# A planned attention and feed-forward kernel: smaller feed-forward steps, other TensorE prices, and a rearranged start

## The chip, the cores and the metric

One NeuronCore of one Trainium2 chip runs the whole program. The metric is the device time of one execution in microseconds (us); lower is better. Three executions of the kernel before took 1087.53, 1088.04 and 1089.18 us, so its median is 1088.04 us. A further execution was profiled; every row below comes from it.

## The reference, cut to what matters

```
scores = scale * q @ k.T                         # 8 batches x 8 heads, 576 tokens, head size 64
scores = where(block_i >= block_j, scores, -1e9) # blocks of 64 tokens
attn   = exp(scores - max(scores)); attn /= sum(attn) + 1e-9
x      = attn @ v                                # (batch, 576, 512)
u      = x + ((x.T @ U) @ V).T                   # U 576 x 32, V 32 x 576
out    = u + relu(u @ w_ch1) @ w_ch2             # 512 -> 2048 -> 512
```

Inputs of the attention and the results are float32; U, V and the two weight matrices arrive as float64.

## The kernel before, in words

**Two stages.** In the first, the 64 heads go through attention one after the other, and 768 of the 2048 hidden columns of the feed-forward part are computed beside them, in 16 chunks of 288 tokens (`ffn_chunk`). In the second stage (`block_products`) the other 1280 hidden columns follow as block products with seven multiplications in place of eight, 3360 TensorE products at L905.

**A head.** SP fetches q and k transposed (`split_qk`); ACT or DVE rounds them into `qa` and `kk`, POOL or DVE makes the remainders `qb` and the second half of `kk`, and two small DMAs copy the halves to the other partitions. Rows 64 to 100 of `qa` and `kk` hold marks of the blocks, so that the mask is part of the product. `maxima` forms the masked scores on TensorE (L1255, L1257), DVE takes their row maxima into `mx` (L1264), TensorE turns `mx` around (L1271), ACT or DVE copies it into `mr`, and a DMA on SP (L1281) lays it into row 96 of `qa`, which subtracts the maximum inside the next product. `probabilities` makes the scores again in three groups (L1300, L1301) and ACT takes their exponential; `apply_v` multiplies with v (L1350 for the first ten heads in float32, L1354 to L1356 afterwards in three 16-bit products); each second head is followed by `mix`, which applies U and V.

**Weights.** `split64` reads 64-bit words by a DMA into a staging buffer `st`, then one ACT, one POOL and three DVE steps make float32 of them. U and V go through it first, then the first 768 columns' w1 (`first_w1`), w2, and all other weights.

**Who sets the order.** Every step of the first and second stage is given to `Plan.add` with an engine, a price in ns, a priority, a function that emits the instructions, and what it reads and writes. `Plan.issue` plays the program with these prices: whenever an engine falls free, it takes the ready step of smallest priority number that it can start. The order found is emitted as it is, and each engine then works through its own list in order; an instruction whose semaphore is not there yet holds up all behind it. Feed-forward products have priorities from 1e6 on, so TensorE takes them when no attention step is ready, in steps of `GM` products of 288 columns. Until 260 us of planned time, `idle` puts products on a tile of zeros (L1495) where TensorE has nothing at all. `START` says when each engine is free for the first time, `VARIANT` seeds a spread of 4% on all prices, and `INTO` is the time that a result takes to reach another engine.

TensorE's steps are priced by `_pe`, for which each product takes its columns, or 109 ns if that is more, with 40 or 60 ns on top in the caller:

```
m = [*m, *[P] * len(ns)][1 : len(ns)] + [P]
return sum(max(0.85 * w, n * COL) for n, w in zip(ns, m))
```

Of the kernel before, what the change touches and what calls it, by code (L numbers as in the profile page):

```python
# [56 lines left out]
START = {"PE": 5000, "DVE": 5600, "ACT": 2750, "POOL": 5500, "SP": 700}  # L57
COL = 0.4555
LA, VA, MP = 1100,700,500
# [13 lines left out]
LIFT = 8  # L73
FW = 10
# [89 lines left out]
class Plan:  # L164
# [8 lines left out]
    def add(self, engine, ns, prio, fn, reads=(), writes=(), hold=(), after=0, port=False, others=(), lazy=False):  # L173

        n = len(self.tasks)
        k = 1 + 0.04 * ((n * 40503 + 7919 * VARIANT) % 65536 / 65536 - 0.5)
# [10 lines left out]
        slots = {b for b in (*reads, *writes) if b.pool is not None}  # L187
# [3 lines left out]
        self.tasks.append(Task(ways, prio, deps, after, slots))  # L191
        if lazy:
            self.tasks[-1].goal = "lazy"

    def issue(self, tc):
# [10 lines left out]
        port, held, last = False, 0, None  # L206
        taken = [False] * len(tasks)
# [13 lines left out]
        while done < len(tasks):  # L221
            for e, q in ready.items():
# [18 lines left out]
                for x in later:  # L241
                    heapq.heappush(q, x)
                spare = [p[-1] for p in self.banks if p]
# [61 lines left out]
def _pe16(*ns):  # L305
    return sum(2.4 + 0.4167 * n for n in ns)


def _pe(*ns, m=()):

    m = [*m, *[P] * len(ns)][1 : len(ns)] + [P]
    return sum(max(0.85 * w, n * COL) for n, w in zip(ns, m))
# [3 lines left out]
def attention_then_mixer(  # L316
# [58 lines left out]
    st_r = ring(fp, 2, [P, GF, 2], I32, "st")  # L375
    z_r = ring(fp, 2, [P, GF], I32, "z")

    def split64(fetches, shape, hi, lo, dst, prio, gate=(), part=slice(None), whole=None):
# [34 lines left out]
        add("SP", max(630 * len(fetches), 2.85 * n), prio, fetch, gate, [st], after=4500 if whole else DL)  # L413
# [12 lines left out]
        add("ACT", _act(n, True), prio, lambda: nc.scalar.copy(hi(), zf), [zt], [dst])  # L426
        add("POOL", 60 + 2.3 * n, prio, lambda: nc.gpsimd.tensor_sub(lo(), zf[part], f32(hi()[part])), [zt, dst], [dst])
# [18 lines left out]
    def power(mu, n, by, sc, prio, pool):  # L446
# [9 lines left out]
            "PE", 150, prio,  # L456
# [579 lines left out]
    nc.scalar.activation(warm.ap, warm.ap, AF.Exp)  # L1036

    for _ in range(9):
        nc.tensor.matmul(banks_f[0][:, 0:P], zero.ap, zero.ap, start=True, stop=True)
# [26 lines left out]
    marks = buf(ap, [P, 2 * W], F32, "marks")  # L1066
# [6 lines left out]
    nc.vector.memset(marks[low], 0.0)  # L1073
    nc.vector.memset(marks[96:101, W : 2 * W], 1.0)
    for n, fill in enumerate((1.0, NEG)):
        x = marks[64:96, n * W : (n + 1) * W].rearrange("p (i h c) -> p i h c", i=5, h=2)
        for h, base in ((1, 0), (0, -5)):
            nc.gpsimd.affine_select(
                out=x[:, :, h, :], in_=x[:, :, h, :], pattern=[[-1, 5], [0, 64]], compare_op=ALU.not_equal,
                fill=fill, base=base, channel_multiplier=1,  # L1080
            )
    make_identity(nc, ident.ap)
    nc.vector.memset(f32(qa_r[0][0:64, 0:64]), 0.0)
    nc.vector.memset(f32(kk_r[0][0:64, :, S:W]), 0.0)
    nc.vector.memset(f32(kk_r[0][64:P, 1, S:W]), 0.0)
    for n in range(2):
        nc.vector.memset(pl_r[n][:, PW - 64 :], 0.0)
        nc.vector.memset(vw(n)[:, :, D : D + 1], 1.0)
    nc.vector.tensor_copy(qa_r[0][low], marks[low, 0:W])
    nc.vector.tensor_copy(kk_r[0][low, 0, :], marks[low, W : 2 * W])  # L1090

    def masked(n, pr):
# [3 lines left out]
        def pads():  # L1096
            nc.gpsimd.memset(f32(qa[0:64, 0:64]), 0.0)
            nc.gpsimd.memset(f32(kk[0:64, :, S:W]), 0.0)
            return nc.gpsimd.memset(f32(kk[64:P, 1, S:W]), 0.0)

        add("POOL", 500, pr, pads, [], [qa.parts[0], *kk.parts])
        for to, x, b in ((qa[low], 0, qa.parts[0]), (kk[low, 0, :], W, kk.parts[0])):
            add(
                "ACT", _act(W, True), pr, lambda to=to, x=x: nc.scalar.copy(to, marks[low, x : x + W]), [], [b],
                others=[("DVE", 64 + 0.55 * W, lambda to=to, x=x: nc.vector.tensor_copy(to, marks[low, x : x + W]), True, 300)],
            )

    def mixing_weights(prio):


        def fetch_u(t):
# [6 lines left out]
            [fetch_u], [P, 4, R], lambda: ust[:, 0:4, 0:R], lambda: ust[:, 0:4, R : 2 * R], ust.parts[0], prio  # L1118
        )
        split64(  # L1120
            [
                lambda t, j=j: nc.sync.dma_start(
                    out=t[64 * j : 64 * (j + 1)], in_=U[512:576, :].rearrange("p (r t) -> p r t", t=2)
                )
                for j in range(2)
            ],
            [P, R], lambda: ust[:, 4, 0:R], lambda: ust[:, 4, R : 2 * R], ust.parts[1], prio,
        )
        for a in (0, T):
            split64(  # L1130
                [
                    lambda t, j=j, a=a: nc.sync.dma_start(
                        out=t[R * j : R * (j + 1)], in_=V[:, 2 * a : 2 * (a + T)].rearrange("p (s t) -> p s t", t=2)
                    )
                    for j in range(3)
                ],
                [3 * R, T], lambda a=a: v3[:, a : a + T], lambda a=a: v3[2 * R :, a : a + T], v3.parts[a // T], prio,
                part=slice(2 * R, 3 * R),
            )

    def split_qk(h, pr):
# [395 lines left out]
```

## Time and profile before

| | us |
|---|---|
| median of three executions | 1088.04 |
| profiled execution | 1086.81 |
| its span, first to last instruction | 1084.9 |
| TensorE busy | 1059.7 (98%) |
| VectorE busy | 965.4 (89%) |
| ScalarE busy | 691.4 (64%) |
| mean granted TensorE clock | 0.997 |

The profiled execution lies 1.9 us over its span and 1.2 us under the median. Matmuls overlap in the pipeline and their ends are modelled, so a TensorE that reads as busy may still lose time between products; the distance from one start to the next tells more than a duration. PE is TensorE's products, PEld its weight loads, DVE VectorE, ACT ScalarE, POOL GpSimd, SP the engine that issues DMAs.

### The profile page before, as it was taken

What the parts mean: (1) busy time and instruction counts of PE and PEld (TensorE: products, weight loads), DVE (VectorE), ACT (ScalarE), POOL (GpSimd) and SP (SyncE); (2) the same over time, 40 slices, a digit from 0 to 9 for tenths busy, and PEclk for the clock granted to TensorE, in tenths of its full rate; (3) what the DMA queues carried; (4) which work ended last, traced back from release to release, by engine and by line L of the source; (5) the groups of instructions that cost most, each with busy time, mean ns of one, the idle gap of its engine ahead of it and who ended that gap; (6) DMA issues with size and microseconds to landing.
All of it is one profiled execution on the core that took longest, in us unless ns stands there. A gap on an engine that the chain in (4) does not pass through costs nothing.

```text
span 1084.9 us, 27041 instructions
## 1 busy us (share of the span) xinstructions
PE 1059.7 (98%) x10325; PEld 891.8 (82%) x10325; DVE 965.4 (89%) x1999; ACT 691.4 (64%) x1435; POOL 405.1 (37%) x509
## 2 busy tenths in 40 slices
PE   9999999999999999999999999999999999999998
PEld 8888888888888878878878877777777777777776
DVE  8899999999999999989988525899998989898987
ACT  5569786777778877867887423455454545455553
POOL 5446566657358886657688330000000000000000
PEclk9899999999999999999999999999999999999999
DMA  8674646565464675555354377040404040313111
GB/s 197 180 198 120 176 118 182 145 190 160 121 193 145 176 220 170 154 171 170 112 174 147 123 264 244 29 132 2 131 1 132 10 123 22 111 34 99 44 46 44
DMA packets 87041, 141.33 MB, mean 130 GB/s; under 512 B 9664, under 2 KB 60800, under 8 KB 86912
## 3 DMA queue, kind: packets, MB, share of 16 engines
q1 hardware_dynamic: 86912, 139.61, 44.3%
q8 instruction: 81, 1.33, 0.5%
q14 instruction: 48, 0.39, 0.1%
HBM read 83.05 MB, written 37.49 MB: 111 GB/s over the span
## 4 chain that ended last, share of the span: by engine, by line
PE 52%; DVE 26%; ACT 6%; DMA 4%; POOL 3%; issue 3%; SPq 0%; DVEq 0%; POOLq 0%; ACTq 0%
PE bb L905 38%; DVE mx L1264 5%; DVE pp L1330 5%; PE bf L612 4%; PE bf L636 3%; DMA vr<-in_v_dram 2%; DVE z L398 2%; DVE hl L620 1%; PE bg L636 1%; DVE wr L406 1%; POOL wr L734 1%; DVE ot L648 1%; DVE x L1369 1%; POOL sg L730 1%; DVE vm L1193 1%
## 5 line engine op out<-in xcount | busy, mean ns | idle before, releaser
L905 PEld LDWEIGHTS <-wb 128*128 128x128 f16 x3360 | 328.7, 98 | 83.2 <-issue 0.3
L905 PE MATMUL bb<-hh,wb 128*128 128x288 f16 x2240 | 370.8, 286 | 0.0
L905 PE MATMUL bb<-hl,wb 128*128 128x288 f16 x1120 | 238.2, 286 | 0.2 <-DVE hl L843 0.2
L834 ACT CAST hh<-hb 128x576 f16<-128x576 f32 (+1 forms) x96 | 56.7, 591 | 66.8 <-PE bb L905 65.6
L636 PE MATMUL bf<-hh,w2h 128*128 128x288 f16 x336 | 96.9, 288 | 0.2 <-DVE hl L620 0.2
L636 PE MATMUL bf<-hh,w2l 128*128 128x288 f16 x336 | 96.2, 286 | 0.0
L636 PE MATMUL bf<-hl,w2h 128*128 128x288 f16 x336 | 96.2, 286 | 0.0
L860 DVE TENSOR_TENSOR wr<-bb,wr 128x576 f32<-128x576 f32 (+1 forms) x120 | 78.0, 654 | 15.7 <-PE bb L905 15.7
L636 PEld LDWEIGHTS <-w2h 128*128 128x128 f16 x768 | 75.1, 98 | 20.5 <-issue 1.3
L612 PEld LDWEIGHTS <-w1h 128*128 128x128 f16 x768 | 72.0, 98 | 21.9 <-issue 4.1
L1264 DVE TENSOR_REDUCE mx<-ba 128x1 f32<-128x320 f32 (+1 forms) x188 | 85.4, 479 | 1.7 <-PE ba L1257 1.6
L1354 PE MATMUL ba<-vv,pp 128*128 128x65 f16 x810 | 85.2, 193 | 0.5 <-DVE tz L1403 0.5
L1355 PE MATMUL ba<-vv,pp 128*128 128x64 f16 x810 | 84.9, 195 | 0.0
L1356 PE MATMUL ba<-vv,pp 128*128 128x65 f16 x810 | 84.2, 192 | 0.2
L1163 POOL TENSOR_TENSOR qb<-raw,qa 64x576 fp32r<-64x576 f32 x48 | 67.5, 1405 | 42.1 <-ACT qa L1156 16.3
L1355 PEld LDWEIGHTS <-pp 128*128 128x128 f16 x810 | 75.3, 97 | 1.7 <-issue 0.7
L1354 PEld LDWEIGHTS <-pp 128*128 128x128 f16 x810 | 74.7, 96 | 2.2 <-issue 0.2
L1356 PEld LDWEIGHTS <-pp 128*128 128x128 f16 x810 | 75.3, 99 | 0.5 <-DVE pp L1330 0.4
L1330 DVE TENSOR_TENSOR pp<-ba,pp 128x512 f16<-128x512 f32 (+1 forms) x107 | 67.5, 643 | 2.8 <-ACT pp L1325 2.8
L612 PE MATMUL bf<-uh,w1l 128*128 128x288 f16 x368 | 69.4, 287 | 0.0
L834 ACT CAST hh<-wr 128x576 f16<-128x576 f32 (+1 forms) x72 | 42.6, 592 | 39.9 <-PE bb L905 39.9
L838 ACT ACTIVATE hh<-ur,sc 128x576 f16<-128x576 f32 x46 | 35.6, 776 | 50.4 <-PE bb L905 28.7
(221 smaller groups left out, 2869.7 us busy)
## 6 DMA issues: line engine op xcount, KB each, us to landing
raw<-in_qk_dram SPq DMA_DIRECT2D x63, 288.0 KB
vr<-in_v_dram SPq DMA_DIRECT2D x32, 320.0 KB
qb<-qa SPq DMA_DIRECT2D x64, 144.0 KB
kk<-kk SPq DMA_DIRECT2D x64, 144.0 KB
o_d<-ot SPq DMA_DIRECT2D x64, 144.0 KB
wr<-o_d SPq DMA_DIRECT2D x32, 288.0 KB
wb<-w_d SPq DMA_DIRECT2D x14, 640.0 KB
out_dram<-wr SPq DMA_DIRECT2D x31, 288.0 KB
```

What stands on the lines that cost most here:

```text
L612: nc.tensor.matmul(ps[:, :T], w()[wn][:, k, fs], m[k].ap, start=(i == 0), stop=(i == len(ops) - 1))
L636: nc.tensor.matmul(ps[:, :T], w()[wn][:, f, ms], hs[f][x].ap, start=(i == 0), stop=(i == len(ops) - 1))
L834: add("ACT", _act(size(x), True), E, lambda: nc.scalar.copy(h(), x[0]()), [x[1]], [hb])
L838: "ACT", _act(size(x), True) + 105, E, lambda: nc.scalar.activation(h(), x[0](), AF.Copy, scale=sc[:, 0:1]), [x[1], sc],
L860: add("DVE", _dve(size(out)), E, lambda: getattr(nc.vector, op)(out[0](), x[0](), y[0]()), [x[1], y[1]], [out[1]])
L905: nc.tensor.matmul(bank[:, i, :T], w(x, k), p.ap[:, k, :], start=first and n == 0, stop=last and n == len(ops) - 1)
L1163: sub = lambda e, dst=dst, x=x, y=y: lambda: e.tensor_sub(dst, raw[:, x], f32(y))
L1264: lambda i=i, view=view: nc.vector.tensor_reduce(out=mx[:, i : i + 1], in_=view(), op=ALU.max, axis=AX.XY if i == 4 else AX.X, negate=True,),
L1330: lambda at=at, view=view, shaped=shaped: nc.vector.tensor_sub(shaped(pl[:, at]), view(), shaped(ph[:, at])),
L1354: nc.tensor.matmul(bank[:, o : o + D + 1], ph[:, w], vv[:, y, 0 : D + 1], start=(j == 0), stop=False)
L1355: nc.tensor.matmul(bank[:, o : o + D], ph[:, w], vv[:, y, D + 1 : 2 * D + 1], start=False, stop=False)
L1356: nc.tensor.matmul(bank[:, o : o + D + 1], pl[:, w], vv[:, y, 0 : D + 1], start=False, stop=(j == i))
```

## The change

**Steps and prices.** `GM` falls from 6 to 2, so a feed-forward step is two products. A TensorE step now has three prices: its own, its weight load, and the length of its last product; a load over `HALF` (40 ns) shows in the plan as far as the last product of the step before does not cover it. The last product of a step counts its columns alone, and the 40 and 60 ns on top become 10. (`open_load(...) > 9999` never holds, so the branch on `WIDE` is not taken.) `VARIANT` goes from 7 to 3, `MP` (priority of U and V) from 500 to 1500, and `START` to earlier times; a weight fetch is planned at 6.0 us instead of 4.5.

**Start.** The first head's q is fetched by SP and its k by ACT's queue, and ACT's table load stands behind that. The tile `marks` goes: the marks are made in head 0's own `qa` and `kk` and copied from there to the two other sets. Staging buffers `st` are three instead of two. V is fetched once, not three times in two halves, and ACT writes it twice. Seven instead of nine products warm TensorE up. For head 0 alone (`RW` = 1), five products turn the five columns of `mx` straight into rows, and two ACT or DVE copies put them into row 96 of `qa`, with no DMA.

```diff
-GM = 6
+GM = 2
-VARIANT = 7
+VARIANT = 3
-START = {"PE": 5000, "DVE": 5600, "ACT": 2750, "POOL": 5500, "SP": 700}
+START = {"PE": 4300, "DVE": 4000, "ACT": 720, "POOL": 3700, "SP": 700}
+HALF, WIDE = 40, 115
-LA, VA, MP = 1100,700,500
+LA, VA, MP = 1100,700,1500
+RW = 1
...
+        def open_load(t):
+            return max(0, t.load - shown) if t.load > HALF else 12 * (shown < 0)
...
+                if n is not None and e == "PE":
+                    ns += open_load(t)
+                    shown = t.last
...
-    m = [*m, *[P] * len(ns)][1 : len(ns)] + [P]
-    return sum(max(0.85 * w, n * COL) for n, w in zip(ns, m))
+    m = [*m, *[P] * len(ns)][1 : len(ns)]
+    return more + sum(max(0.85 * w, n * COL) for n, w in zip(ns, m)) + ns[-1] * COL, 0.85 * P, ns[-1] * COL
...
-    st_r = ring(fp, 2, [P, GF, 2], I32, "st")
+    st_r = ring(fp, 3, [P, GF, 2], I32, "st")
...
-        add("SP", max(630 * len(fetches), 2.85 * n), prio, fetch, gate, [st], after=4500 if whole else DL)
+        add("SP", max(630 * len(fetches), 2.85 * n), prio, fetch, gate, [st], after=6000 if whole else DL)
...
-    for _ in range(9):
+    for _ in range(7):
...
-        for a in (0, T):
-            split64(
-                [
-                    lambda t, j=j, a=a: nc.sync.dma_start(
-                        out=t[R * j : R * (j + 1)], in_=V[:, 2 * a : 2 * (a + T)].rearrange("p (s t) -> p s t", t=2)
-                    )
-                    for j in range(3)
-                ],
...
+        split64(
+            [lambda t: nc.sync.dma_start(out=t, in_=V.rearrange("p (s t) -> p s t", t=2))], [R, S],
+            [lambda: v3[0:R, :], lambda: v3[R : 2 * R, :]], [lambda: v3[2 * R :, :]], v3.parts, prio,
+        )
...
+        if h == 0:
+            for e, d, a, b in (("SP", nc.sync, 0, halves[0]), ("ACT", nc.scalar, S, halves[1])):
+                add(e, 600, -6000.0, lambda d=d, a=a: d.dma_start(out=raw[:, a : a + S], in_=qk[h, :, a : a + S]), writes=[b], after=2400)
...
-            add("PE", _pe(*ns) + 40, pr, products, [qa.parts[0], kk.parts[0]], [bank])
+            add("PE", _pe(*ns, more=10), pr, products, [qa.parts[0], kk.parts[0]], [bank])
...
+        if h < RW:
+            wide, one = Buf(pool=early), Buf(pool=early)
+
+            def turned():
+                for i in (4, 0, 3, 2, 1):
+                    o = wide[0:1, P * (i - 1) : P * i] if i else one[0:1, 0:P]
+                    nc.tensor.transpose(out=o, in_=mx[:, i : i + 1], identity=ident.ap)
...
-            add("PE", _pe(*ns) + 60, pr, products, [*qa.parts, *kk.parts, *qb.parts], [bank])
+            narrow = [m for j, *_ in tiles for m in (P, P)]
+            add("PE", _pe(*ns, m=narrow, more=10), pr, products, [*qa.parts, *kk.parts, *qb.parts], [bank])
```

**What moves.** Three places of the orders show it. On SP, in the first heads, from the fetch of V (`st<-in_V`) to the first block of w1 (`st<-in_w1`), before:

```order
L1132 DMA st0_99<-in_V_dram 32x576 x3
L1281 DMA qa1_153<-mr1_168 1x5x128
L1132 DMA st1_100<-in_V_dram 32x576 x3
L1168 DMA qb2_160<-qa2_154 64x576
L1168 DMA kk2_157<-kk2_157 64x576
L1168 DMA qb0_158<-qa0_152 64x576
L1168 DMA kk0_155<-kk0_155 64x576
L1148 DMA raw1_150<-in_qk_dram 64x1152
L1148 DMA raw2_151<-in_qk_dram 64x1152
L1281 DMA qa2_154<-mr0_167 1x5x128
L1148 DMA raw0_149<-in_qk_dram 64x1152
L492 DMA st0_99<-in_w1_dram 128x768
```

The same place of the change:

```order
L1154 DMA st2_101<-in_V_dram 32x1152
L1186 DMA qb1_157<-qa1_151 64x576
L1186 DMA kk1_154<-kk1_154 64x576
L1169 DMA raw0_147<-in_qk_dram 64x1152
L1193 DMA vr0_167<-in_v_dram 128x640
L1193 DMA vr1_168<-in_v_dram 128x640
L1169 DMA raw1_148<-in_qk_dram 64x1152
L1315 DMA qa1_151<-mr1_166 1x5x128
L1186 DMA kk2_155<-kk2_155 64x576
L1186 DMA qb2_158<-qa2_152 64x576
L521 DMA st0_99<-in_w1_dram 128x768
```

Six fetches of a part of V become one, head 0's `qa<-mr` is gone, and the first block of w1 is issued right after the copies of head 2; before, the copies of head 3 and three more fetches of q and k stood ahead of it.

On ACT, in the first heads, from the copy of v (`vv<-vr`) to the first exponential of head 0 (`pp0<-bw`), before:

```order
L1182 COPY vv1_172<-vr1_170 128x10x64
L1275 ACTIVATE mr0_167<-ba3_97 5x128
L1275 ACTIVATE mr1_168<-ba1_95 5x128
L426 CAST ust_187<-z0_101 128x4x32
L426 CAST ust_187<-z1_102 128x32
L1104 CAST qa2_154<-marks_189 64x640
L1156 CAST kk2_157<-raw2_151 64x576
L1314 ACTIVATE pp0_161<-bw_98 128x640
```

The same place of the change:

```order
L1200 COPY vv1_170<-vr1_168 128x10x64
L441 ACTIVATE z0_102<-st0_99 128x128
L441 ACTIVATE z1_103<-st1_100 64x32
L1299 ACTIVATE qa0_150<-ba0_94 1x512
L1299 ACTIVATE qa0_150<-ba1_95 1x128
L1132 CAST qa2_152<-qa0_150 32x640
L1174 CAST kk2_155<-raw2_149 64x576
L1174 CAST qa2_152<-raw2_149 64x576
L1349 ACTIVATE pp0_159<-bw_98 128x640
```

ACT writes head 0's row straight into `qa0` (L1299) where it wrote `mr0` (L1275), and the casts into `ust` stand behind the exponential.

On TensorE, at head 34's second group (`qa1,kk1` of 448 columns; `w1` and `w2` rows are feed-forward products), before:

```order
L612 LDWEIGHTS w1l_221
L612 MATMUL bf0_89<-uh0_123,w1l_221 128x288
L612 LDWEIGHTS w1l_221
L612 MATMUL bf0_89<-uh1_124,w1l_221 128x288
L1300 MATMUL ba2_96<-qa1_153,kk1_156 128x448
L1301 MATMUL ba2_96<-qb1_159,kk1_156 128x448
L1255 MATMUL bw_98<-kk2_157,qa2_154 128x288 x2
L1257 MATMUL bw_98<-kk2_157,qa2_154 128x64
```

The same group in the change:

```order
L1273 MATMUL bw_98<-kk2_155,qa2_152 128x288 x2
L1275 MATMUL bw_98<-kk2_155,qa2_152 128x64
L665 LDWEIGHTS w2l_214
L665 MATMUL bf1_90<-hh_209,w2l_214 128x288
L665 LDWEIGHTS w2h_213
L665 MATMUL bf1_90<-hl_210,w2h_213 128x288
L1334 MATMUL ba0_94<-qa1_151,kk1_154 128x448
L1335 MATMUL ba0_94<-qb1_157,kk1_154 128x448
```

Before, the group stands behind a run of two feed-forward steps of six and right ahead of the next head's maxima; now one feed-forward pair stands between these two attention steps.

Counted over the whole orders: feed-forward products stand in 208 runs between attention steps before and in 279 now; 438 of the 2304 stood behind the last attention step and 370 do now; of the products on zeros, 58 stood ahead of head 0's first group (L1300) and 40 do now, and 146 stand in either order in all. Ahead of head 11's first group stood 6 feed-forward products and stand 44 now.

## Rows read from the trace of the kernel before

**Rows 1.** Page, busy time, whole span (us, share, instructions).

```profile
PE 1059.7 (98%) x10325; PEld 891.8 (82%) x10325; DVE 965.4 (89%) x1999; ACT 691.4 (64%) x1435; POOL 405.1 (37%) x509
```

**Rows 2.** Busy time by stretch: from:to, length, then PE, PEld, DVE, ACT, POOL, PEclk, DMA.

```profile
20.00:40.00 20.00, 17.89 (x130) 17.37 (x130) 15.17 (x36) 9.85 (x22) 8.83 (x11) 0.85 0.78 185
160.00:200.00 40.00, 38.42 (x448) 33.49 (x447) 37.94 (x90) 29.64 (x67) 25.48 (x30) 1.00 0.62 176
700.00:800.00 100.00, 100.00 (x818) 79.84 (x817) 92.62 (x149) 51.71 (x87) 0.00 (x0) 1.00 0.23 72
```

**Rows 3.** Chain that ended last, two late pieces: start us, length us, what.

```profile
618.92 6.62 PE bf L612 x54
...
672.28 409.41 PE bb L905 x3342
```

**Rows 4.** Waits of PE from 100 to 600 us: total us, times, longest.

```profile
PE bw L1255 <- DVE pp L1330: 4.5, 10, 1.3
```

**Rows 5.** Instructions in order of time, head 0's maxima to its first group.

```profile
8.30 1.28 DVE L1264 TENSOR_REDUCE mx<-ba 128x1 f32<-128x448 f32 x3
...
10.73 0.27 PE L1271 MATMUL ba<-ident,mx 128*5 128x128 f32 x1
...
11.46 1.28 DVE L1264 TENSOR_REDUCE mx<-ba 128x1 f32<-128x448 f32 x3
11.54 0.83 SPq L1281 DMA_DIRECT2D qa<-mr  x1
...
15.02 0.41 PE L1300 MATMUL bw<-qa,kk 128*128 128x320 f32 x1 [0.16 <-DMA qa<-mr]
```

**Rows 6.** Instructions in order of time, the first block of w1.

```profile
26.85 0.75 SPq L492 DMA_DIRECT2D st<-in_w_dram  x1
...
30.34 0.54 ACT L414 ACTIVATE z<-st 128x384 f32<-128x384 f32 x1 [2.49 <-DMA st<-in_w_dram]
...
30.97 0.70 ACT L1314 ACTIVATE pp<-bw 128x640 f32<-128x640 f32 x1
...
31.72 0.53 PE L1255 MATMUL bw<-kk,qa 96*128 96x288 f32 x2 [2.11 <-ACT pp L1314]
```

**Rows 7.** Busy time by stretch of 2 us around and behind that wait.

```profile
30.00:32.00 2.00, 0.28 (x2) 0.28 (x3) 0.21 (x1) 1.67 (x5) 0.97 (x2) 1.00 1.04 328
...
34.00:36.00 2.00, 2.00 (x17) 2.00 (x16) 1.93 (x3) 0.17 (x1) 0.78 (x1) 0.52 0.54 114
36.00:38.00 2.00, 2.00 (x12) 2.00 (x10) 1.12 (x3) 0.82 (x3) 1.35 (x2) 0.50 0.19 40
38.00:40.00 2.00, 2.00 (x10) 1.96 (x10) 1.51 (x5) 0.30 (x1) 0.06 (x1) 0.50 0.53 151
```

**Rows 8.** PE's products in order of time around 302 to 305 us.

```profile
302.44 0.19 PE L1257 MATMUL bw<-kk,qa 96*128 96x64 f32 x1
302.47 0.45 PE L1300 MATMUL ba<-qa,kk 128*128 128x448 f32 x1
302.76 0.36 PE L1301 MATMUL ba<-qb,kk 128*128 128x448 f32 x1
302.96 0.31 PE L1300 MATMUL ba<-qa,kk 128*128 128x320 f32 x1
...
304.81 0.29 PE L636 MATMUL bf<-hl,w2h 128*128 128x288 f16 x1
304.84 0.46 PE L1257 MATMUL ba<-kk,qa 96*128 96x448 f32 x1
305.14 0.30 PE L636 MATMUL bf<-hh,w2h 128*128 128x288 f16 x1
```

**Rows 9.** Groups of DVE's instructions by line and shape: count, busy us, mean ns.

```profile
L1157 DVE CAST qa<-raw 64x576 fp32r<-64x576 f32 x25 | 14.1, 563 | 1.5 <-PE ba L1300 1.5
...
L1384 DVE TENSOR_TENSOR xl<-x,xh 128x512 fp32r<-128x512 f32 x12 | 9.6, 802 | 0.7 <-ACT t L1406 0.5
L1276 DVE TENSOR_SCALAR mr<-ba 5x128 fp32r<-5x128 f32 x17 | 4.5, 267 | 0.1
```

More of the change, by code (lines that the diff above doesn't have):

```diff
@@ L175, in add @@
         n = len(self.tasks)
+        load = last = 0
+        if isinstance(ns, tuple):
+            ns, load, last = ns
         k = 1 + 0.04 * ((n * 40503 + 7919 * VARIANT) % 65536 / 65536 - 0.5)
@@ L186, in add @@
         deps.discard(n)
-        slots = {b for b in (*reads, *writes) if b.pool is not None}
+        slots = [*dict.fromkeys(b for b in (*reads, *writes) if b.pool is not None)]
         for b in slots:
@@ L191, in add @@
         self.tasks.append(Task(ways, prio, deps, after, slots))
+        self.tasks[-1].load, self.tasks[-1].last = load, last
         if lazy:
@@ L242, in issue @@
                     heapq.heappush(q, x)
+                if n is not None and e == "PE" and open_load(tasks[n]) > 9999:
+                    wide = min((x for x in q if not taken[x[1]] and tasks[x[1]].last > WIDE and free(tasks[x[1]])), default=None)
+                    if wide:
+                        q.remove(wide)
+                        heapq.heapify(q)
+                        heapq.heappush(q, (tasks[n].prio, n))
+                        n = wide[1]
+                        t = tasks[n]
+                        ns, fn, shared, late = t.ways[e]
+                        new = [b for b in t.slots if b.ap is None]
+                if n is not None and e == "PE":
+                    ns += open_load(t)
+                    shown = t.last
                 spare = [p[-1] for p in self.banks if p]
@@ L1072, in attention_then_mixer @@
     low = slice(64, P)
[L1073 to L1080, printed above, removed]
-            )
+    rows = slice(64, 96)
+    one_hot, barred = f32(qa_r[0].ap), f32(kk_r[0][:, 0, :])
+    nc.vector.memset(one_hot[low], 0.0)
+    x = qa_r[0].ap[rows].rearrange("p (i h c) -> p i h c", i=5, h=2)
+    for h, base in ((1, 0), (0, -5)):
+        nc.gpsimd.affine_select(
+            out=x[:, :, h, :], in_=f32(x[:, :, h, :]), pattern=[[-1, 5], [0, 64]], compare_op=ALU.not_equal,
+            fill=1.0, base=base, channel_multiplier=1,
+        )
     make_identity(nc, ident.ap)
-    nc.vector.memset(f32(qa_r[0][0:64, 0:64]), 0.0)
+    nc.vector.memset(barred[96:P], 0.0)
+    nc.vector.memset(barred[96:101], 1.0)
+    nc.vector.memset(one_hot[0:64, 0:64], 0.0)
     nc.vector.memset(f32(kk_r[0][0:64, :, S:W]), 0.0)
     nc.vector.memset(f32(kk_r[0][64:P, 1, S:W]), 0.0)
+    nc.vector.tensor_scalar_mul(kk_r[0][rows, 0, :], one_hot[rows], NEG)
     for n in range(2):
@@ L1164, in split_qk @@
             add(
-                "POOL", 1340, pr, sub(nc.gpsimd), [raw, a], [b], others=[("DVE", 68 + 1.042 * S, sub(nc.vector), True, 600)],
+                "POOL", 1340, pr, sub(nc.gpsimd), [raw, a, r], [b], others=[("DVE", 68 + 1.042 * S, sub(nc.vector), True, 600)],
             )
@@ L1199, in split_v @@
         add(
-            "PE", 150, pr,
+            "PE", (109, 109, 109), pr,
             lambda: nc.tensor.transpose(
@@ L1356, in products @@
                         nc.tensor.matmul(bank[:, o : o + D + 1], pl[:, w], vv[:, y, 0 : D + 1], start=False, stop=(j == i))
-            add("PE", (240 if h < FW else 92) * sum(i + 1 for i in tiles) + 20, pr, products, [vv, *ph.parts[:some], *pl.parts[:some]], [bank], hold=[xb])
+            add("PE", ((240 if h < FW else 92) * sum(i + 1 for i in tiles), 109 if h < FW else 30, 27), pr, products, [vv, *ph.parts[:some], *pl.parts[:some]], [bank], hold=[xb])
         def inverse():
```

86 lines of the change are left out of this document (44 added, 42 removed).

## The prediction

> **What bounds the kernel now.** The page's first line comes first: TensorE is busy for 1059.7 us of the span, 98%, and VectorE for 89% [rows 1]. The busy time by stretch then shows that there are two stages with different limits [rows 2]. From 700 to 800 us TensorE alone is full. From 160 to 200 us both are: PE has 38.42 us of 40, DVE 37.94. In the first 40 us neither is: PE has 17.89 us of 20 at a mean clock of 0.85, DVE only 15.17. The chain of waits, last, says what the end hangs on [rows 3]: 3342 block products in one piece of 409.41 us, 122.5 ns each, and ahead of them a piece of 54 feed-forward products in 6.62 us, 122.6 ns each. These are feed-forward products that attention left over. So the end is the sum of all of TensorE's work plus the time that it loses before the last 409 us. The 2304 feed-forward products and the 3360 block products are the same in both kernels; a gain can only be TensorE time that was lost and is now used.
>
> TensorE's losses are of three kinds. The first is the start, before any feed-forward product may run: nothing can fill a gap there, so what is lost is lost for good. The second are waits for a late result. The third are weight loads that no product covers. All three appear below.
>
> **The first head's maxima.** The last of head 0's maxima ends at 8.30 + 1.28 = 9.58 us, yet its first group starts at 15.02, released by the DMA of the row [rows 5]: the turn at 10.73 stands behind products of head 1, the issue is at 11.54, and the landing is 3.5 us later. The change replaces this by five products and two copies on ACT. One such product takes 0.27 us alone [rows 5], and five that overlap I put at 0.7; the two copies read 640 elements together, for which an exponential takes 0.70 us in one piece [rows 6], so some 0.9 in two. Head 0 alone would then be ready at 9.58 + 0.7 + 0.9 + 0.2 for the hand-overs = 11.4 us. But the order of the change puts head 1's turn ahead of head 0's first group, and it needs head 1's maxima, which ended at 11.46 + 1.28 = 12.74 [rows 5]. With the raw data of head 1 asked for somewhat earlier I take 12.5 us: **2.5 us gained**. The ends are 1.9 (head 1 no earlier: 12.74, its turn of 0.27 and the hand-over, 13.1) and 3.6 us (11.4). The rest of the new start goes with it: the marks on DVE and POOL keep their sizes about, two warming products and some zeros are gone but lay beside the fetch of q, so I cost them at nothing; if the fetch were not the cover, they would be worth under a microsecond.
>
> **The first block of w1.** Its fetch is issued at 26.85 us; ACT reaches the first step on it too early and stands for 2.49 us, until 30.34 [rows 6]. Behind it on ACT, in order, stand the exponentials, and TensorE waits 2.11 us for their bank [rows 6]. From 30 to 32 us TensorE does 0.28 us of work and DVE 0.21, while the DMA engines move 328 GB/s [rows 7]. And a bill follows: from 34 to 40 us the granted clock is 0.52, 0.50 and 0.50 [rows 7], the 1.2 GHz level, with TensorE busy throughout; work that takes 6 us there takes 3.0 at 2.4 GHz. What happened before it fell is the empty stretch at 30 us. So this one wait costs 2.1 + up to 3.0 = 5.1 us. The change reads V once in place of three times, which takes 288 KB of 432 out of SP's queue ahead of it, some 0.9 us at 328 GB/s; it issues w1's first block right after head 2's copies, at least five DMAs sooner; it gives a third staging buffer and plans 6.0 us for this landing, so that ACT's list has more work ahead of the step. I take **3 us gained**, because other steps crowd into the same stretch; the ends are 0 (the wait stands somewhere else) and 5.1.
>
> **Feed-forward steps of two.** Where TensorE has a queue of feed-forward work, a ready attention step waited for the rest of a step of six, up to 6 × 122.5 = 735 ns; now for up to 245 ns. What this is worth shows in two ways. First, the loads. Behind a product of 64 columns that itself takes 0.03 us (302.44 to 302.47), a product of 448 columns takes 0.29 us to the next start, where the next one of the same width takes 0.20: 0.09 us of its load shows [rows 8]. Behind a feed-forward product the same width has 304.81 to 305.14, 0.33 us for both, which is 0.12 + 0.20: nearly nothing shows [rows 8]. In the changed order some 60 more attention steps stand behind a feed-forward pair; many of them stood behind 192 or 448 columns before, which cover most of a load themselves, so I put 25 of them at 0.08: **2 us gained**, with ends of 0 and 60 × 0.09 = 5.4. The Trainium skill, "TensorE: Matmul & The Clock Gate", section "Step-by-step: what each phase is for", says that TensorE pulls weight loads ahead of products in flight, so that the next tile's load runs beside this tile's product; taken as a full cover, no load would show and this term would be 0, the forecast 1080.5. The 0.09 us above speak against a full cover: a load is hidden only as far as one product is long.
>
> Second, the fill. 438 feed-forward products were left when attention ended, now 370: 68 × 122.5 ns = 8.3 us less remain at the end. That is a gain only where these 68 stand in time that TensorE lost; where it was full, attention ends later by as much. From 160 to 200 us 1.58 us of 40 are idle, 4%, and part of it is waits for DVE: 4.5 us in 10 cases for the exponentials' halves alone [rows 2, 4]. TensorE's prices without the 40 and 60 ns on top, and with 29 in place of 109 ns for a last narrow product, let the plan put feed-forward products where it formerly believed TensorE still busy. I take **2 us** beyond the loads; the ends are 0 and 8.3 in all for loads and fill together.
>
> **DVE and ACT.** DVE sets the pace of attention, so its list counts. It loses 9 casts of q of 563 ns (5.1 us) but gains 9 copies of `mr` of 267 (2.4) and 3 remainders `xl` of 802 (2.4) [rows 9]; the other shifts nearly cancel. I cost this at nothing. The casts go to ACT, busy for 64% [rows 1], which covers them unless it stands ahead of exponentials.
>
> **Sum.** 2.5 + 3 + 2 + 2 = 9.5 us from 1086.8 gives 1077.3 for a run like the profiled one. The median before is 1.2 us above that, so **1078.5 us**. With all terms at their lower end but one or two of them the time is 1084 to 1087; at their upper ends, 3.6 + 5.1 + 8.3 = 17, it is 1071.
>
> **The rivals.** (1) *The attention steps come too early: slower.* TensorE works in order. The larger steps and the extra 40 to 60 ns were slack: an attention step stood on average some 0.25 us later than now (half of four products). Now 279 runs of feed-forward work end at an attention step where 208 did. If its inputs from DVE or ACT are late against the plan, TensorE stands in front of them with feed-forward work behind it. For it: DVE is nearly full from 160 to 200 us [rows 2], and a wait of this kind took 0.45 us [rows 4]. Against it: TensorE's waits before were few. The point of decision is 9.5 us over 279 entries, 34 ns each; at 0.06 us for each of them the cost is 16.7 us and the time 1078.5 + 16.7 = 1095. (2) *Nothing moves.* Attention is paced by DVE, and the time saved in the first 40 us comes back as a wait for w1, whose eight blocks come no earlier; the 68 products only change places with attention steps. For it: DVE at 37.94 of 40 and unchanged in its sum. Against it: in the order of the change 44 feed-forward products stand ahead of head 11's first group, 6 before, so w1 is not later by heads. It gives 1088 less at most 2: 1087. (3) *The clock falls again.* With 40 instead of 58 products on zeros ahead of head 0's first group, an early wait may leave TensorE empty for 2 us, as at 30 us [rows 7], and another 3 us go at 1.2 GHz: 1078.5 + 2 + 3 = 1083.5, still faster. (4) *All of it holds*, with DVE's waits going too: 1071.
>
> **How the numbers follow.** A measurement of this kernel tells 0.2%, 2.2 us, from no change. The forecast, 1075 to 1083, has 0.42; (4) 0.12; (3) 0.12; (2) 0.14; (1) 0.20. Faster is the forecast, (3) and (4), 0.66; same is (2), 0.14; slower is (1), 0.20. The range leaves out less than 0.1 of (4) and the upper half of (1): 1068 to 1094.
>
> **What would show it.** Right: head 0's first group starts near 12.5 us; no wait of 2 us on `st<-in_w` around 30 us and no stretch at 1.2 GHz after it; the block products still take 122.5 ns and start about 9 us sooner than 672.28; feed-forward products left over when attention ends fill some 45 us. Wrong: waits of PE for DVE or ACT well over those of before (rival 1), or the same start of the long block piece although the first 40 us are shorter (rival 2).

## The result, and the profile after

The changed kernel took 1069.61 us (median; 1069.45 to 1071.94), the kernel before, run beside it, 1087.78 us (1082.11 to 1089.18). The ratio is 0.9848, with a 95% interval of 0.9810 to 0.9885: 18.2 us less, where 9.5 were forecast. The direction and the range held; the size of the terms did not.

Page of the changed kernel, busy time over its span of 1067.5 us; it answers to [rows 1]:

```profile
PE 1051.5 (99%) x10325; PEld 887.8 (83%) x10325; DVE 964.2 (90%) x2001; ACT 693.2 (65%) x1432; POOL 403.8 (38%) x507
```

The same 10325 products are in it. DVE's sum is 1.2 us lower: its list cost nothing, as forecast. Busy time by stretch of the changed kernel (from:to, length, then PE, PEld, DVE, ACT, POOL, PEclk, DMA), against [rows 2]:

```profile
20.00:40.00 20.00, 19.74 (x168) 19.15 (x167) 17.32 (x43) 13.56 (x31) 12.38 (x14) 1.00 0.77 187
80.00:100.00 20.00, 18.15 (x101) 16.43 (x100) 14.73 (x38) 14.02 (x33) 13.39 (x13) 0.67 0.33 87
160.00:200.00 40.00, 39.92 (x497) 35.31 (x496) 39.04 (x97) 30.63 (x71) 28.64 (x32) 1.00 0.66 176
700.00:800.00 100.00, 100.00 (x819) 79.88 (x817) 92.26 (x148) 51.85 (x87) 0.00 (x0) 1.00 0.22 68
100.00:600.00 500.00, 494.89 (x5839) 430.36 (x5839) 479.89 (x1130) 400.41 (x907) 335.20 (x416) 1.00 0.57 161
```

The last of these stretches in the kernel before:

```profile
100.00:600.00 500.00, 485.95 (x5619) 420.05 (x5618) 474.76 (x1116) 395.04 (x894) 339.62 (x415) 1.00 0.57 161
```

Three things are to be seen. From 20 to 40 us the clock is 1.00 and PE has 19.74 us where it had 17.89. From 160 to 200 us its idle time falls from 1.58 to 0.08 us although DVE was nearly full already; over 100 to 600 us it falls from 14.05 (500 − 485.95) to 5.11 us, and 220 more products fit in. And there is one new loss: from 80 to 100 us the clock is 0.67.

Chain that ended last in the changed kernel, two places between 599 and 700 us (start us, length us, what), against [rows 3]:

```profile
599.71 6.39 PE bf L641 x52
...
606.82 0.09 PE ba L1451
...
609.00 8.09 PE bf L665 x66
...
653.10 46.92 PE bb L934 x383
```

The products still follow each other every 122.5 ns (46.92 / 383; 8.09 / 66 = 122.6), and the long block piece starts at 653.10 instead of 672.28, 19.2 us sooner. To its end it has 3354 products in 410.88 us, against 3342 in 409.41 before; the 12 more stood ahead of it before. So the block products end 17.7 us sooner, at 1063.98 instead of 1081.69. The last product of attention proper, the one at 606.82, stood at 615.76 before: attention itself ends 8.9 us sooner, and with fewer feed-forward products left over, 370 against 438.

Waits of PE for another engine, 100 to 600 us, changed kernel (total us, times, longest), against [rows 4]:

```profile
PE ba L1391 <- DVE pp L1365: 1.8, 2, 1.3
PE bf L641 <- DVE hl L649: 1.4, 1, 1.4
PE bf L665 <- DVE hl L649: 0.5, 2, 0.3
```

All waits in this list come to 4.8 us, against 12.3 before. The wait of the maxima for DVE's halves, 4.5 us in 10 cases, is gone.

### The profile page after: what moved, and what is told of

Same layout as the page of the kernel before. It is cut to its first block, busy times and chain, and to the rows that moved or that the text cites. A ratio compares the mean times of both kernels' runs of the same rounds, so it can differ in the third digit from the quotient of the medians.

```text
span 1067.5 us, 27013 instructions
## 1 busy us (share of the span) xinstructions
PE 1051.5 (99%) x10325; PEld 887.8 (83%) x10325; DVE 964.2 (90%) x2001; ACT 693.2 (65%) x1432; POOL 403.8 (38%) x507
## 4 chain that ended last, share of the span: by engine, by line
PE 80%; DVE 12%; DMA 3%; ACT 2%; POOL 2%; issue 2%; SPq 0%; POOLq 0%; DVEq 0%; ACTq 0%
PE bb L934 39%; PE bf L665 10%; PE bf L641 9%; DVE mx L1282 2%; PE ba L1334 2%; DVE pp L1365 2%; PE ba L1275 2%; PE ba L1335 2%; PE ba L1390 2%; PE ba L1389 2%; PE ba L1391 2%; PE bw L1335 2%; PE bw L1334 1%; PE bw L1273 1%; PE ba L1448 1%
## 5 line engine op out<-in xcount | busy, mean ns | idle before, releaser
L665 PE MATMUL bf<-hh,w2h 128*128 128x288 f16 x372 | 106.4, 287 | 0.5 <-DVE hl L649 0.5
L665 PE MATMUL bf<-hh,w2l 128*128 128x288 f16 x372 | 106.5, 287 | 0.0
L665 PE MATMUL bf<-hl,w2h 128*128 128x288 f16 x372 | 106.3, 287 | 0.0
L665 PEld LDWEIGHTS <-w2h 128*128 128x128 f16 x768 | 72.9, 98 | 19.0 <-issue 1.7
L641 PEld LDWEIGHTS <-w1h 128*128 128x128 f16 x768 | 69.8, 98 | 19.1 <-issue 2.6
L1282 DVE TENSOR_REDUCE mx<-ba 128x1 f32<-128x320 f32 (+2 forms) x188 | 84.6, 476 | 1.1 <-PE ba L1275 0.9
L1334 PE MATMUL ba<-qa,kk 128*128 128x320 f32 (+1 forms) x191 | 67.3, 358 | 2.8 <-DVE mx L1282 1.8
L1365 DVE TENSOR_TENSOR pp<-ba,pp 128x512 f16<-128x512 f32 x107 | 67.2, 644 | 0.6 <-ACT pp L1360 0.2
L1181 POOL TENSOR_TENSOR kk<-raw,kk 64x576 fp32r<-64x576 f32 x44 | 62.9, 1429 | 11.4 <-DVE kk L1175 2.2
```

The source lines that it names most:

```text
L641: nc.tensor.matmul(ps[:, :T], w()[wn][:, k, fs], m[k].ap, start=(i == 0), stop=(i == len(ops) - 1))
L665: nc.tensor.matmul(ps[:, :T], w()[wn][:, f, ms], hs[f][x].ap, start=(i == 0), stop=(i == len(ops) - 1))
L1181: sub = lambda e, dst=dst, x=x, y=y: lambda: e.tensor_sub(dst, raw[:, x], f32(y))
L1282: lambda i=i, view=view: nc.vector.tensor_reduce(out=mx[:, i : i + 1], in_=view(), op=ALU.max, axis=AX.XY if i == 4 else AX.X, negate=True,),
L1334: nc.tensor.matmul(o, kk[:, 0, ks], qa[:, 64 + q0 : 64 + q1], start=True, stop=False)
L1365: lambda at=at, view=view, shaped=shaped: nc.vector.tensor_sub(shaped(pl[:, at]), view(), shaped(ph[:, at])),
```

## The start in the changed kernel: two gains, and one given back

Chain of waits of the changed kernel, 6 to 14 us:

```profile
6.13 6.61 DMA st<-in_U_dram
12.75 0.02 issue
12.77 0.02 ACT z L441
12.80 0.23 issue
13.03 0.03 ACT qa L1299
13.06 0.46 issue
13.52 0.26 ACT qa L1299
```

And the instructions concerned, in order of time:

```profile
9.88 0.71 PE L1293 MATMUL ba<-ident,mx 128*1 128x128 f32 x5
...
12.77 0.23 ACT L441 ACTIVATE z<-st 64x32 f32<-64x32 f32 x1 [1.09 <-DMA st<-in_U_dram]
13.03 0.74 ACT L1299 ACTIVATE qa<-ba 1x512 fp32r<-1x512 f32 x2
...
13.82 0.41 PE L1334 MATMUL bw<-qa,kk 128*128 128x320 f32 x1 [1.59 <-ACT qa L1299]
```

The prices were right: five products 0.71 us (0.7 in the sum), two copies 0.74 (0.9). What the sum left out is the place on ACT: the copies stand behind a step on U that waits 1.09 us for a DMA of 6.61 us. The products were done at 10.59; the copies began at 13.03. So head 0's first group starts at 13.82 and not near 12.5.

The first block of w1 is no longer waited for. Before, its fetch was issued at 23.55 (the issue at 26.85 in [rows 6] is that of the second block):

```profile
23.55 0.54 SPq L492 DMA_DIRECT2D st<-in_w_dram  x1
```

The last signal of its landing came at 30.25, just ahead of ACT's step at 30.34. In the changed kernel it is issued at 16.51, the last signal comes at 22.26, and ACT's step runs at 23.62 without idle time before it:

```profile
16.51 0.55 SPq L521 DMA_DIRECT2D st<-in_w_dram  x1
...
23.62 0.55 ACT L441 ACTIVATE z<-st 128x384 f32<-128x384 f32 x1
```

The first group of head 9 comes at 79.2 us instead of 86.9. But by head 12 little of the lead is left: its first group starts at 122.5 against 122.4, with 108 feed-forward products done ahead of it against 96, which is 1.5 us of work (12 × 122.5 ns). Two instructions of the changed kernel around 84 us, in order of time:

```profile
83.70 0.36 PE L1335 MATMUL bf<-qb,kk 128*128 128x448 f32 x1
85.91 0.41 PE L1334 MATMUL ba<-qa,kk 128*128 128x320 f32 x1 [1.85 <-DVE mx L1282]
```

and its busy time by stretch there and behind it:

```profile
84.00:86.00 2.00, 0.15 (x2) 0.10 (x1) 1.97 (x5) 1.98 (x5) 1.05 (x2) 1.00 0.88 252
86.00:88.00 2.00, 2.00 (x12) 1.92 (x12) 1.80 (x7) 1.98 (x6) 1.18 (x2) 0.70 0.62 178
88.00:90.00 2.00, 2.00 (x12) 1.94 (x12) 1.62 (x4) 2.00 (x7) 1.99 (x3) 0.50 0.66 136
...
98.00:100.00 2.00, 2.00 (x12) 1.45 (x11) 1.97 (x4) 1.79 (x5) 0.97 (x1) 0.50 0.30 63
```

Head 10's second group waits 1.85 us until DVE has taken a row maximum (`mx`) out of the bank that its next product writes; just ahead of that maximum DVE works for 0.36 and 0.68 us on the weights (L536, L472). TensorE is empty, and the clock then stands at the 1.2 GHz level for 13.7 us, from 86.8 on, though TensorE is busy throughout. This is rival (3), at another place than it named. What stood at 30 us before [rows 7] was cured, and came back at 85.

## The experiments

Between them the runs undo the four parts of the change: the start (with `START` and `MP`), TensorE's prices, the steps of two (`GM`), and the seed (`VARIANT`), which shifts all prices by its own draw. "Idle" below is 500 us less PE's busy time from 100 to 600 us in the view by stretch.

### From before to after, one part at a time

**Seed alone** (`e7_before_seed3`, the kernel before):

```diff
-VARIANT = 7
+VARIANT = 3
```

> The kernel before with VARIANT = 3, the seed of after; nothing else. If seeds only scatter the time: 1083 to 1093. If the new seed is a good part of the gain: 1072 to 1081. Against the run with the new start alone (1080.2) it tells what of those 8 us is the start.

1088.85 us (1085.82 to 1093.03), ratio 1.0023 [0.9999, 1.0048]. The seed gives nothing by itself in the kernel before.

**Seed and start** (`e4_start_alone`, the changed kernel with the steps and prices of before; the price lines that follow are taken back, with the callers' 40 and 60 ns and the prices of TensorE's other steps, such as 150 in place of 109 ns for a transpose):

```diff
-GM = 2
+GM = 6
...
-            return max(0, t.load - shown) if t.load > HALF else 12 * (shown < 0)
+            return max(0, t.load - shown) if t.load > HALF else 0
...
-    m = [*m, *[P] * len(ns)][1 : len(ns)]
-    return more + sum(max(0.85 * w, n * COL) for n, w in zip(ns, m)) + ns[-1] * COL, 0.85 * P, ns[-1] * COL
+    m = [*m, *[P] * len(ns)][1 : len(ns)] + [P]
+    return sum(max(0.85 * w, n * COL) for n, w in zip(ns, m))
```

> The kernel after with GM = 6 and the prices as before: the new start and the new seed alone. A and B: 1081 to 1088, less if no clock falls around head 10 (then 1079 to 1082). C: 1068 to 1075.

1080.16 us (1078.68 to 1086.19), ratio 0.9945 [0.9915, 0.9974]; idle 9.59 us. The start is worth 8.7 us (1088.85 − 1080.16), and its interval does not touch the one of the seed alone.

**Seed, start and prices** (`e1_steps_of_six`, the changed kernel):

```diff
-GM = 2
+GM = 6
```

> The kernel after with GM back at 6: new start, new prices, new seed stay. Theory A (the steps of two bring the 8.9 us by which attention ends sooner and the 8.3 us of feed-forward products placed earlier): most is lost again, 1081 to 1087. Theory B (the prices of TensorE's steps bring it): 1070 to 1074. Theory C (another seed and luck of the order): 1068 to 1075.

1072.56 us (1070.84 to 1076.81), ratio 0.9868 [0.9827, 0.9909]; idle 4.97 us. The prices give 7.6 us more, with steps of six; theory A is out, B and C both allow for the time. From here the steps of two add 3.0 us, which the two intervals do not tell apart. After 600 us this kernel loses 2.60 us of TensorE (80 − 77.40), where the changed kernel loses nothing:

```profile
600.00:680.00 80.00, 77.40 (x636) 61.89 (x635) 41.47 (x80) 27.75 (x57) 11.80 (x19) 1.00 0.58 204
```

The reason stands below, with `f2_six_seed7`.

**Seed, start and steps of two, without the prices** (`e2_old_prices`, the changed kernel): the price lines of `e4_start_alone` are taken back, `GM` stays 2.

> The kernel after with TensorE's prices as before (40 and 60 ns on top, 109 ns for a narrow last product, no loads): new start, steps of two and seed stay. Theory A: 1069 to 1075. Theory B: 1081 to 1087. Theory C: 1068 to 1075.

1085.71 us (1084.17 to 1086.46), ratio 0.9976 [0.9955, 0.9997]. Of the theories only B allows for this time and the one of `e1_steps_of_six`. Here the steps of two cost 5.5 us over `e4_start_alone` and the prices are worth 16.1. Busy time by stretch of this kernel:

```profile
100.00:600.00 500.00, 488.35 (x5688) 416.13 (x5686) 472.38 (x1126) 399.91 (x900) 331.48 (x407) 1.00 0.56 158
```

Idle is 11.65 us, and 1716 of the 2304 feed-forward products stand ahead of attention's end, against 1934 in the changed kernel: a feed-forward step of two is no gain while the plan believes that attention steps last longer than they do.

**Prices and steps, without the start** (`e3_old_start`): the kernel before with the changed `_pe`, `open_load` and `GM = 2`, and `VARIANT = 7`.

> The kernel before with the new prices and steps of two; start, START, MP, staging buffers and seed as before. The profile says that the start's 7.7 us at head 9 are gone at head 12, where the clock had fallen: if that holds here too, A and B both say 1068 to 1075. If the start is worth its 7.7 us in the end, 1076 to 1081.

1080.54 us (1076.23 to 1087.78), ratio 0.9933 [0.9905, 0.9961]; idle 8.60 us. In the profile the clock falls three times, at 17.5, 58.5 and 567 us; the four of its ten executions at a mean clock of 0.997 or more took 1076.2 to 1078.8.

### How much the prices do

**Attention's steps dearer** (`e8_dear_steps`, the changed kernel; 100 ns more on each step of maxima and probabilities):

```diff
-            add("PE", _pe(*ns, more=10), pr, products, [qa.parts[0], kk.parts[0]], [bank])
+            add("PE", _pe(*ns, more=110), pr, products, [qa.parts[0], kk.parts[0]], [bank])
...
-            add("PE", _pe(*ns, m=narrow, more=10), pr, products, [*qa.parts, *kk.parts, *qb.parts], [bank])
+            add("PE", _pe(*ns, m=narrow, more=110), pr, products, [*qa.parts, *kk.parts, *qb.parts], [bank])
```

> The kernel after with each step of maxima and probabilities priced 100 ns dearer (110 instead of 10 on top), six such steps a head. If too high prices of TensorE's steps make it run ahead of its plan and stand in waits: the waits of PE over 130 ns from 100 to 600 us go from 8 us back to 17 or more, and the time to 1080 to 1088. If the shown loads or the last narrow product were what mattered, and not the level of the prices: 1067 to 1074.

1095.09 us (1090.63 to 1100.34), ratio 1.0062 [1.0033, 1.0091], above both ranges. In the profiled execution the clock falls at 15.6 us for 13.7 us, and twice later; executions at a mean clock of 0.997 still took 1090.6 to 1090.9, so the clock is the smaller part of it.

**The seed of before** (`e6_after_seed7`, the changed kernel with `VARIANT = 7`):

> The kernel after with VARIANT = 7, the seed of before; nothing else. If seeds only scatter the time: within 5 us of after, 1065 to 1075. If the new seed is a good part of the gain: 1077 to 1086.

1065.73 us (1064.95 to 1066.40), ratio 0.9785 [0.9770, 0.9799]. There is no hole at 84 us and the clock is 1.00 throughout. The seed thus makes 3.9 us in the changed kernel, and with the hole filled (`e5_clock_kept`, below) the two seeds are 1.1 us apart. Against `e3_old_start`, which has the same seed, prices and steps, the start is worth 14.8 us.

**Loads free in the plan** (`f1_loads_free`, the changed kernel with `VARIANT = 7`):

```diff
-            return max(0, t.load - shown) if t.load > HALF else 12 * (shown < 0)
+            return 0
```

> The kernel after with seed 7 (1065.7 us, no fall of the clock) and open_load at 0: the plan takes every weight load as hidden, so it believes TensorE faster than it is by what shows (15 us from 100 to 600 us). If the pricing of shown loads is a real part of the gain: 1070 to 1078. If only too dear prices hurt and too cheap ones do not: 1064 to 1068.

1062.10 us (1061.88 to 1064.56), ratio 0.9750 [0.9730, 0.9770]: the fastest of all, and under both ranges. Busy time by stretch, first of `e8_dear_steps`:

```profile
100.00:600.00 500.00, 486.85 (x5645) 415.41 (x5645) 474.54 (x1118) 402.32 (x909) 342.17 (x412) 0.99 0.57 159
```

then of `e6_after_seed7`:

```profile
100.00:600.00 500.00, 494.75 (x5792) 429.44 (x5791) 471.14 (x1118) 401.63 (x908) 337.89 (x415) 1.00 0.58 163
```

and of `f1_loads_free`:

```profile
100.00:600.00 500.00, 499.01 (x5899) 436.80 (x5897) 467.21 (x1104) 408.16 (x923) 343.23 (x420) 1.00 0.58 163
```

Idle is 13.15, 5.25 and 0.99 us, in the order of the prices; the eight runs with the change's own prices, whatever their start, steps and seed, lie between 3.69 and 8.62. Ahead of attention's end stand 1662, 1904 and 1964 feed-forward products. `f1_loads_free` has two waits left in PE's list of 100 to 600 us:

```profile
PE bf L641 <- DVE hl L649: 0.4, 2, 0.2
PE bw L1273 <- DVE pp L1365: 0.3, 1, 0.3
```

So the model of shown loads, which the change adds, is not what pays; in the one order that ignores them the time is better, by 3.6 us, which is no more than a seed makes. What pays is that TensorE is priced low. The idle time and the counts fit this reading: the plan then believes that TensorE is through early and puts feed-forward products ahead of attention steps whose inputs really come later. With dear steps it believes TensorE still busy, and on the chip TensorE stands.

### What steps of two do at the end of attention

**Steps of six, seed 7** (`f2_six_seed7`, the changed kernel with `VARIANT = 7` and `GM = 6`):

> The kernel after with seed 7 and GM = 6. With seed 3 the steps of six cost 3 us, some of it hidden by a shorter fall of the clock. If steps of two are worth what the shown loads of over 20 ns differ by (15.0 against 17.1 us): 1067 to 1069. If nothing: 1065 to 1066. If the steps are worth what the old prices made of them: 1072 or more.

1075.01 us (1074.58 to 1076.36), ratio 0.9865 [0.9847, 0.9884], 9.3 us over `e6_after_seed7`. The time lies in the third range, for a reason that the expectation does not name. Idle from 100 to 600 us is alike, 5.82 against 5.25. Most of the difference stands behind it, in the chain of waits of this kernel, 609 to 625 us:

```profile
609.95 2.97 PE bf L665 x24
...
612.94 0.52 DVE ot L677
...
613.49 1.66 DMA o_d<-ot
...
617.17 0.50 POOL us L624
...
620.06 0.44 ACT uh L629
620.50 0.04 issue
620.54 4.33 PE bf L641 x21
```

and in its busy time by stretch:

```profile
616.00:620.00 4.00, 0.59 (x3) 0.19 (x2) 0.00 (x0) 0.60 (x2) 3.35 (x6) 1.00 0.77 215
600.00:680.00 80.00, 74.77 (x609) 58.86 (x606) 37.50 (x74) 24.45 (x51) 11.79 (x19) 0.98 0.60 205
```

The last stretch in `e6_after_seed7`:

```profile
600.00:680.00 80.00, 79.84 (x653) 63.60 (x651) 45.05 (x86) 29.44 (x56) 9.66 (x16) 1.00 0.57 194
```

The feed-forward products that do not need the last batch number 2016 of 2304. Here 1974 of them were done when attention ended, 1904 in `e6_after_seed7`. The queue runs dry before the last batch has come through DVE, a DMA, POOL and ACT, and TensorE does 0.59 us of work in four. From 600 to 680 us it is idle for 5.23 us against 0.16, and from 620.4 us the clock is at the 1.2 GHz level for 3.4 us, half of which is lost; 2.5 of the 9.3 us stay without a place. With 1934, as in the changed kernel, nothing is lost there; PE is idle for 2.60 us with 1956 (`e1_steps_of_six`), 2.13 with 1958 (`f4_staging_of_two`) and 1.46 with 1964 (`f1_loads_free`). So what filling the gaps can give ends here, unless the last batch's chain is shortened, which was not tried.

### The parts of the start

**The row by DMA again** (`f3_row_by_dma`, the changed kernel with `VARIANT = 7`):

```diff
-RW = 1
+RW = 0
```

> The kernel after with seed 7 and RW = 0: head 0's row goes by mr and a DMA again. The forecast put this part at 2.5 us; the traces show head 0's first group 1.2 us earlier. If that lead lasts to the end: 1067 to 1068.5. If it is lost in the first heads: 1065 to 1066.5.

1070.41 us (1070.21 to 1071.55), ratio 0.9824 [0.9803, 0.9845]: above both ranges and 4.7 us over `e6_after_seed7`, both with the clock at 1.00. Head 0's first group in `f3_row_by_dma`:

```profile
16.98 0.31 PE L1334 MATMUL bw<-qa,kk 128*128 128x320 f32 x1
```

and in `e6_after_seed7`:

```profile
13.64 0.42 PE L1334 MATMUL bw<-qa,kk 128*128 128x320 f32 x1 [1.12 <-ACT qa L1299]
```

The row is worth 3.3 us at head 0, and 1.3 more by the end.

**Two staging buffers and a landing planned at 4.5 us** (`f4_staging_of_two`, the changed kernel with `VARIANT = 7`):

```diff
-    st_r = ring(fp, 3, [P, GF, 2], I32, "st")
+    st_r = ring(fp, 2, [P, GF, 2], I32, "st")
...
-        add("SP", max(630 * len(fetches), 2.85 * n), prio, fetch, gate, [st], after=6000 if whole else DL)
+        add("SP", max(630 * len(fetches), 2.85 * n), prio, fetch, gate, [st], after=4500 if whole else DL)
```

> The kernel after with seed 7, two staging buffers st instead of three and the weight fetch planned at 4.5 us instead of 6.0. If these two took away the wait on the first block of w1: TensorE or ACT stands 2 us around 25 to 35 us again, the clock falls behind it, 1068 to 1073. If V's single fetch and the new order on SP did it: 1065 to 1067.

1069.73 us (1067.19 to 1073.08), ratio 0.9817 [0.9786, 0.9848]: 4.0 us over `e6_after_seed7`. In the profiled execution the clock falls at 68.9 us for 10.2 us; of the others, two at a mean clock of 1.00 took 1067.2 and 1067.4. At the same clock the two settings are therefore worth some 1.5 us, and the profiled execution loses more than that, 2.13 us, in a queue that ran dry after 600 us. ACT's wait ahead of the first block of w1 did come back:

```profile
25.94 0.55 ACT L441 ACTIVATE z<-st 128x384 f32<-128x384 f32 x1 [1.78 <-POOL qb L1181]
```

The step reads `st` and not `qb`, and the last signal of its block's fetch came at 25.84. TensorE does not stand for it: it has 2.00 us of 2 from 24 to 26 and from 26 to 28 us, and the clock stays at 1.00 there. So these two settings hold ACT's wait off, but they are not what took the wait from TensorE.

### What the fall of the clock costs

**The hole filled** (`e5_clock_kept`, the changed kernel; the first product of head 10's second group is made ten times, with the same result each time):

```diff
+                    for _ in range(9 if (h, g) == (10, 1) else 0):
+                        nc.tensor.matmul(o, kk[:, 0, ks], qa[:, 64 + q0 : 64 + q1], start=True, stop=True)
```

> The kernel after; the order is the same, but the first product of head 10's second group is made ten times instead of once (nine more of 448 columns, about 1.84 us), so that TensorE is not empty from 84.1 to 85.9 us. If the empty stretch there brings the 13.7 us at 1.2 GHz, the clock stays at 2.4 GHz and up to 6.9 us come back: 1063 to 1066. If DVE, ACT and the split of w1 set that stretch anyway, the clock stays up and the time does not: 1068 to 1070.

1064.67 us (1064.40 to 1065.13), ratio 0.9776 [0.9761, 0.9790], 4.9 us under the changed kernel. Its busy time by stretch:

```profile
84.00:86.00 2.00, 1.97 (x11) 1.49 (x9) 1.97 (x5) 1.97 (x5) 1.02 (x2) 1.00 0.91 271
86.00:88.00 2.00, 2.00 (x17) 1.92 (x17) 1.93 (x8) 1.98 (x6) 1.23 (x2) 1.00 0.58 162
```

Nine products more, 1.85 us of work for nothing (83.48 to 85.33), give back 4.9 us: TensorE then does 17 products from 86 to 88 us where the changed kernel does 12. Head 12 starts at 117.7 instead of 122.5.

## Why the prediction was right, and where it was mis-sized

The four parts add up in the order seed, start, prices, steps: 1087.78 → 1088.85 → 1080.16 → 1072.56 → 1069.61. That is +1.1, −8.7, −7.6 and −3.0 us. These medians carry the clock with them: `e7_before_seed3`, `e4_start_alone` and `e1_steps_of_six` at a mean clock of 0.997 or more have medians of 1086.9, 1080.1 and 1070.9, and the changed kernel with its hole filled has 1064.7. At a like clock the start is thus worth 6.8 us, the prices 9.2 and the steps of two 6.2. Of these 6.2, 2.60 are idle time after 600 us, 2.1 are shown loads (below), and 1.7 are half of the 3.4 us that the clock is at the 1.2 GHz level from 85.7 us on in the profile of `e1_steps_of_six`.

**The bound** held: the gain is TensorE time that was lost before the long block piece. Block products take 122.5 ns in either kernel, and they end 17.7 us sooner; of the 19.2 us by which the long piece starts sooner, 1.5 go to the 12 products more in it.

**Head 0's row**, 2.5 us forecast: 1.2 in the trace of the changed kernel at head 0 (15.02 to 13.82), 3.3 to 4.7 by the run that undoes it. The term's prices held to 0.2 us; the queue on ACT was not counted.

**The first block of w1**, 3 forecast: the wait and the 1.2 GHz stretch are gone. The prediction took the second block's issue (26.85) for the first one's (23.55). So its fetch had 6.7 us from issue to landing, not the 3.5 that these rows seem to give, and has 5.75 now; it is issued 7.0 us sooner, and ACT comes to its step only after the landing. Together with the row the lead was 7.7 us at head 9, more than the 5.5 forecast for both. Most of it was then given back by rival (3), the clock, whose price was forecast at 5 (2 + 3) and measured at 4.9. Its place was not foreseen. The start as a whole, 8.7 with the old prices and 14.8 with the new ones and seed 7 (partly falls of the clock: 6.8 and 12.0 by the executions at 0.997 or more), was under-sized; of the 14.8 the row has 4.7 and staging 4.0 (1.5 at the same clock), and the rest was not taken apart.

**Loads**, 2 forecast. Worked out from the starts of successive products: each is given its own time by its columns (109 ns for a transpose), laid end to end behind the one ahead, and where the next start comes later than that, a gap of 20 to 130 ns counts as a load: 302 such gaps before, 20.1 us, and 239 after, 15.0 us, from 100 to 600 us. So 5.1 us, near the upper end of 5.4. The steps of two have only part of it: the sum is 21.6 us in `e4_start_alone`, 17.1 in `e1_steps_of_six` and 15.0 in the changed kernel, so 4.5 go with the prices and 2.1 with the steps. The Trainium skill, "TensorE: Matmul & The Clock Gate", section "Step-by-step: what each phase is for", has the next tile's weights load while this tile's product runs. The 15.0 us that still show speak against taking this as a full cover.

**Fill** is the step that failed in size: "I take 2 us beyond the loads; the ends are 0 and 8.3 in all for loads and fill together". Gaps over 130 ns, worked out in the same way, fell from 50 with 22.4 us to 19 with 8.3: 14.1 us. With the loads that is 19, of which 4 were forecast (and the hole at 84 us took some of it back). The bound of 8.3 rested on the 68 products that were no longer left over, as if attention could not end sooner. It ended 8.9 us sooner as well. The reason was wrong in part too: a ready attention step that waits less for a shorter feed-forward step explains little, since with the old prices the steps of two were 5.5 us slower, and with the new ones they gained 3.0 (6.2 at a like clock) with no less idle time from 100 to 600 us (4.97 with steps of six, 5.11 with two). The prices carry the gain, 7.6 or 16.1 us: these waits are 16.9 us in `e4_start_alone`, 7.5 in `e1_steps_of_six` and 8.3 in the changed kernel. The prediction names the prices in one sentence behind the steps.

**Rivals.** (1), attention steps that come too early, fell: the runs of feed-forward work rose from 208 to 279 and the waits fell from 12.3 to 4.8 us. Its direction was backwards: slack in the prices makes TensorE wait, as `e8_dear_steps` shows at 1095.09 us, with 24.3 us in such waits. (2) held for the start alone and only in this order: most of the lead of head 9 was gone at head 12, through the clock; w1's blocks have a part in it only by DVE's 1.0 us on the weights right ahead of the hole. (4), 1071, is the nearest to the time measured, though not by its sum: the falling clock took 4.9 us from a gain of 23.

**Luck.** The time lies within the range because two misses pull against each other, the fill that was too small and the fall of the clock. The same order with its hole filled (1064.67 us) and the same kernel with the old seed (1065.73) would both have lain below 1068. The 0.2% that a measurement was to tell from no change was too narrow as well: executions of the kernel before lie between 1082.1 and 1091.8 us.

**What stays open**: why the plan with seed 3 leaves the hole at 84 us and that with seed 7 does not; and what `f1_loads_free` would give with the last batch's chain made shorter. Three versions beat both kernels: `f1_loads_free` (1062.10 us), `e5_clock_kept` (1064.67) and `e6_after_seed7` (1065.73).

## What to carry to other kernels

Where an order is planned from prices and then fixed, test the prices of the engine that has filler work in both directions: too dear and the chip finds it idle, too cheap and the filler lies where the waits would be. Before calling a short wait of TensorE harmless, look at the granted clock of the next 15 us. And count what filler is left that does not depend on the last result: when it runs dry, the gain turns into one long wait.

## What the runs showed of the hardware that was not expected

One empty stretch of 1.85 us was followed by 13.7 us at 1.2 GHz with TensorE busy all the time; in the kernel before, 2.11 us were followed by 6.8 us. The stretch at the lower level is thus not in proportion to the gap.

Executions of one and the same kernel differ mostly by the clock: those of the kernel before with a mean granted clock of 0.996 to 1.00 took 1082.1 to 1086.8 us, those with 0.989 to 0.995 took 1087.3 to 1091.8. Orders without a hole in the first 100 us (`e5_clock_kept`, `e6_after_seed7`, `f3_row_by_dma`) lay within 1.5 us each, at 1.00 throughout.
